# A fused attention, mixture-of-experts and gated-network kernel: two unused tiles that shift SBUF addresses, and raw weight loads issued one step earlier

## The chip, the cores and the metric

The kernel runs on one core of one Trainium2 chip. The metric is the device time of one execution in microseconds (us). Several executions were timed, and one execution was also recorded by the hardware profiler; the rows below come from that one.

## What is computed

Three stages follow each other, with float32 inputs and outputs, except that weights of the last network lie in HBM as 64-bit floats.

```python
# 1. attention: 4 batches, 8 heads, 512 local and 32 global positions, head size 64
s_g = scale * q_g @ concat(k_g, k_l).T ; out_g = softmax(s_g) @ concat(v_g, v_l)
s_l = concat(scale * q_l @ k_g.T, where(|i - j| <= 32, scale * q_l @ k_l.T, -1e9))
out_l = softmax(s_l) @ concat(v_g, v_l)
x = concat(out_g, out_l) as (4, 544, 512)
# 2. mixture of 8 experts, one expert per token, 512 -> 1024 -> 512
e = argmax(logits[b, s]) if s == 0 or local_gate[b, s] < 0.5 else previous e
out[b, s] = p[e] * (relu(x[b, s] @ w1[e]) @ w2[e])
# 3. network with a gate, 512 -> 1024 -> 512
h = relu(x @ w_in)
gate = sigmoid(conv_out)      # depthwise, 3 taps along the sequence
return (h * gate) @ w_out
```

## The kernel before

Attention fills about the first 160 us, the mixture of experts the time to about 430 us, the last network the rest. Large products are done in three passes: each float32 operand is split into a high part (suffix h) and a residual (suffix l), and PE multiplies high by high, high by residual and residual by high. A split is a cast on ACT (line 1043 for weights) and a subtraction on DVE (line 1044 for weights, line 1101 for tokens). Three lines hold 432 such matmuls of full tiles each (144 for each pass): L1108 (first layer of an expert, stationary xh or xl), L1124 (second layer of an expert, stationary gh or gl) and L1625 (second layer of the last network, stationary fh or fl). 128 rows of a stationary operand lie at the same byte address in 128 partitions.

**The mixture of experts** sorts the tokens by expert into slots of at most 128, 25 at most; `Moe.step(s)` (line 1405) handles one slot, `Moe.run` (line 1185) calls it for s = 2 to 20. A step does, in this order: first layer of slot s (`layer1`), the load of the next first-layer weights (`fetch(s, 1)`, 2 MB, only if the expert changes), a gather of tokens for slot s+3, the transposition of the tokens of slot s+1, the finishing operation of a conversion that waits (line 1017), the split of the next first-layer weights (`resplit(s + 1, 1)`), a conversion (only if the expert does not change), second layer of slot s-1 (`layer2`), the load of the next second-layer weights (`fetch(s - 1, 2)`, 2 MB, under the same condition), the transposition of the hidden values of slot s, the split of the second-layer weights (`resplit(s, 2)`), and a conversion (if the expert changes). Slots with few tokens take a short path through the unsplit weights, `few`. The conditions are read from memory at run time and appear as branches (L1294, L1303).

**The raw pieces.** The weights of the last network arrive as 64-bit floats in 16 pieces of 128 rows by 4 KB (0.52 MB each). `raw_load` (line 1441) puts a piece into one half of the tile fx, the halves by turns; `convert` calls `conv64` (lines 1006 to 1017), which makes float32 of it by integer operations: six on DVE (L1010 to L1015, 128 x 512 each), one on POOL (L1016), and the finishing one on DVE (L1017), deferred to the next step. In the kernel before, piece s-3 is loaded at the head of step s and converted in step s.

**Queues.** All these loads are issued by SP, in program order; an issue that has to wait holds up everything behind it on SP. Weight loads go to the tiles ws1 (first layer) and ws2 (second layer). `Ffn2.open` (line 1485) makes the tiles of the last network, the main function at line 1716 those of constants.

Of the kernel before, what the change touches and what calls it, by code (L numbers as in the profile page):

```python
# [8 lines left out]
F32 = mybir.dt.float32  # L9
F32R = mybir.dt.float32r  # L10
BF16 = mybir.dt.bfloat16
I32 = mybir.dt.int32
# [5 lines left out]
P = 128  # L18
# [69 lines left out]
class Attn:  # L88
    def __init__(self, ctx, cr, cs, tc, q_l, k_l, v_l, q_g, k_g, v_g, wcat, wz, ident, x_dram, L, late, hook):
        self.tc, self.nc = tc, tc.nc  # L90
        nc = tc.nc
        self.q_l, self.k_l, self.v_l, self.q_g, self.k_g, self.v_g = q_l, k_l, v_l, q_g, k_g, v_g
        self.wcat, self.ident, self.x_dram, self.L, self.late, self.hook = wcat, ident, x_dram, L, late, hook
        self.lgt, self.wz = {}, wz
# [247 lines left out]
    def evac(self, c, ps, tag, w=P):  # L342
# [4 lines left out]
        if c < B:  # L347
            j = 4 * c + c // 2
            nc.vector.tensor_copy(self.L[:, j:j + 4, :], t.rearrange("p (i e) -> p i e", e=32)[:, :, 0:9])
        else:  # L350
            nc.vector.tensor_copy(self.L[0:w, 8, :], t[0:w, 0:9])

# [207 lines left out]
NA = 2  # L560
# [95 lines left out]
class Routing:  # L656
    def __init__(self, nc, c, pool, ident, L):
        self.nc, self.c, self.ident, self.L = nc, c, ident, L
        self.m = pool.tile([P, NT], F32, name="r_m")
# [275 lines left out]
    def few(self, b0, first):  # L935
# [3 lines left out]
        v.scalar_tensor_tensor(sm, b0, -128.0, first[0:1], ALU.mult, ALU.add)  # L939
        v.tensor_scalar(sm, sm, P - TS - 0.5, 1024.0, ALU.is_lt, ALU.mult)  # L940
        v.tensor_tensor(sm, sm, b0, ALU.add)
# [37 lines left out]
        v.tensor_tensor(self.gate, pg, rx, ALU.mult)  # L979


TS = 32
NTS = P // TS
NWARM_M = 10
# [21 lines left out]
def conv64(nc, raw, out):  # L1006
    hi, lo = raw[:, :, 1], raw[:, :, 0]
    v = nc.vector
    a = out.bitcast(I32)
    v.tensor_scalar(a, hi, 3, 0x7FFFFFFF, ALU.logical_shift_left, ALU.bitwise_and)  # L1010
    v.scalar_tensor_tensor(a, hi, -2 ** 31, a, ALU.bitwise_and, ALU.bitwise_or)
    v.tensor_scalar(hi, hi, 1, 21, ALU.logical_shift_left, ALU.logical_shift_right)
    v.tensor_scalar(hi, hi, 897.0, -1.0, ALU.is_ge, ALU.mult)
    v.scalar_tensor_tensor(a, lo, 29, a, ALU.logical_shift_right, ALU.bitwise_or)
    v.tensor_scalar(lo, lo, 28, 1, ALU.logical_shift_right, ALU.bitwise_and)  # L1015
    nc.gpsimd.tensor_tensor(a, a, lo, ALU.add)  # L1016
    return lambda: v.scalar_tensor_tensor(a, a, 0x40000000, hi, ALU.bitwise_xor, ALU.bitwise_and)  # L1017
# [33 lines left out]
class Moe:  # L1051
    def __init__(self, sig, tc, W, ident, x_dram, y_dram, rt, w1, w2, wi, wo):
        self.nc, self.tc = tc.nc, tc
        self.W, self.ident, self.x_dram, self.y_dram = W, ident, x_dram, y_dram
        self.rt, self.w1, self.w2, self.wi, self.wo = rt, w1, w2, wi, wo
        self.sig = sig
        self.xs, self.xt, self.ht, self.hs, self.next, self.chg, self.sm = {}, {}, {}, {}, {}, {}, {}
        self.conv = []

    def open(self, ctx):  # L1060
        self.ctx = ctx
        self.tp = ctx.enter_context(self.tc.tile_pool(name="m_tp", bufs=2))
        self.ps = ctx.enter_context(self.tc.tile_pool(name="m_ps", bufs=2, space=PSUM))
        self.ys = [self.tp.tile([P, DM], F32, name=f"ys{i}", bufs=1) for i in range(2)]
# [243 lines left out]
    def turn_x(self, s):  # L1308
# [13 lines left out]
        def raw():  # L1322
            nc.scalar.copy(xs[:, 0:NKC * TS].rearrange("p (k t) -> p k t", t=TS), t[:, :, P - TS:P])  # L1323

# [15 lines left out]
    def layer1(self, s):  # L1340
# [4 lines left out]
        def few():  # L1345
            w = FF // NTS
            for k in range(NKC):
                for j in range(NTS):
                    nc.tensor.matmul(hp[0][TS * j:TS * j + TS, 0:w], xs[:, TS * k:TS * k + TS], W.s[1][:, k, w * j:w * j + w],
                                     start=k == 0, stop=k == NKC - 1)  # L1350
# [31 lines left out]
    def layer2(self, s):  # L1382
# [5 lines left out]
        def few():  # L1388
            for k in range(NFC):
                j, a = divmod(k, n)  # L1390
                for i in range(NTS):
                    nc.tensor.matmul(yp[TS * i:TS * i + TS, 0:w], hs[:, P * (n + a) + TS * j:P * (n + a) + TS * j + TS],
                                     W.s[2][:, k, w * i:w * i + w], start=k == 0, stop=k == NFC - 1)
            for i in range(NTS):
                nc.scalar.copy(y[P - TS:P, w * i:w * i + w], yp[TS * i:TS * i + TS, 0:w])

# [7 lines left out]

    def step(self, s):
        W, hi = self.W, NSLOT - 3
        if NA < s <= NA + 16:
            self.raw_load(s - NA - 1)
        if s + 1 < hi - 1:
            self.small(s + 1)  # L1410
        self.layer1(s)
        self.fetch(s, 1)
        if s + 3 < hi:
            self.xs[s + 3] = self.gather(s + 3)
        if s + 1 < hi - 1:
            self.turn_x(s + 1)
        else:
            self.xt[s + 1] = self.hi_lo_t(self.xs.pop(s + 1), NKC, "x")
        while self.conv:
            self.conv.pop()()  # L1420
        self.resplit(s + 1, 1)
        if NA < s <= NA + 16:
            with self.tc.If(self.chg[s + 1] == 0):
                self.convert(s - NA - 1)
        if s == NA:
            for _ in self.rest:
                pass
        else:
            self.layer2(s - 1)
            self.fetch(s - 1, 2)  # L1430
        self.turn_h(s)
        self.resplit(s, 2)
        if NA < s <= NA + 16:
            self.conv.pop()
            with self.tc.If(self.chg[s + 1] != 0):
                self.convert(s - NA - 1)
# [2 lines left out]
        return (1, s // 2, 512 * (s % 2)) if s < 8 else (2, s - 8, 0)  # L1439

    def raw_load(self, s):
        self.raw = self.f2.fx[s % 2].bitcast(I32).rearrange("p (n t) -> p n t", t=2)
        n, k, o = self.chunk(s)
        src = (self.wi, self.wo)[n - 1]
        self.nc.sync.dma_start(self.raw.rearrange("p n t -> p (n t)"), src[P * k:P * k + P, 2 * o:2 * o + 1024])

    def convert(self, s):
        n, k, o = self.chunk(s)
        self.conv.append(conv64(self.nc, self.raw, self.W.f[n][:, k, o:o + 512]))


class Ffn2:
# [32 lines left out]
    def open(self, ctx):  # L1485
        nc, tc = self.nc, self.tc
        self.tp = ctx.enter_context(tc.tile_pool(name="f_tp", bufs=2, reuse_waits="tile"))
        self.ps = ctx.enter_context(tc.tile_pool(name="f_ps", bufs=2, space=PSUM, reuse_waits="tile"))
        self.hp = [self.tp.tile([P, S + 2], F32, name=f"f_hp{i}", bufs=1) for i in range(3)]
        for t in self.hp:  # L1490
            nc.gpsimd.memset(t[:, 0:1], 0.0)
            nc.gpsimd.memset(t[:, S + 1:S + 2], 0.0)
        self.n = 0
# [207 lines left out]
def moe_kernel(ctx, tc, q_l, k_l, v_l, q_g, k_g, v_g, w_gate, w_local, w1, w2, w_in, conv_w, w_out, out):  # L1701
    nc = tc.nc
    outf = out.rearrange("b s d -> (b s) d")
    with tc.manual_schedule():
        cp = ctx.enter_context(tc.tile_pool(name="const", bufs=1))
# [8 lines left out]
        warm = cp.tile([P, 1], F32, name="warm")  # L1714
        nc.scalar.activation(warm, ident[:, 0:1], AF.Exp)
        L = cp.tile([P, NT, 9], F32, name="L")
        cc = Consts()

        def late():
# [142 lines left out]
```

## Time and profile before

| what | value |
|---|---|
| time, median of 3 runs | 636.39 us (634.14 to 636.82) |
| the profiled execution | 638.55 us |
| its span in the profile | 636.6 us |
| mean granted clock of TensorE | 0.979 |
| busy: PE, PEld, DVE, ACT, POOL | 92%, 77%, 66%, 50%, 27% of the span |

The span is what the profiler recorded between the first and the last instruction; the execution's own time is 1.95 us longer. PE is the engine of matmuls, PEld its loads of stationary operands, DVE, ACT and POOL are VectorE, ScalarE and GpSimd, SP issues DMAs; a q behind a name (PEq, DVEq, SPq) is the engine's sequencer, which handles branches, waits and issues. [...]

### The profile page before, as it was taken

Reading aid. Unit: us, or ns where it says so; the run is one execution under the profiler, and the core shown is the slowest. Engines: PE = TensorE matmul, PEld = TensorE weight load, DVE = VectorE, ACT = ScalarE, POOL = GpSimd, SP = SyncE. Lnnn points to the kernel's source line nnn. Section 1 sums busy time; section 2 is a strip of 40 time slices with the busy share of each in tenths; the row PEclk is TensorE's granted clock in tenths of the full one; section 3 lists DMA queues with packets and bytes.
Section 4 is the critical chain, followed back from the end, with each engine's and each line's share of the span. In section 5 each row is a group of like instructions: output and inputs, shape, how many; then the busy total and the mean of one; then the engine's idle time right before and its main releaser. Section 6 shows DMA issues by size and latency. Waiting matters only on the chain. (4 is left out here: it accounts for less than half of the span.)

```text
span 636.6 us, 16330 instructions
## 1 busy us (share of the span) xinstructions
PE 587.8 (92%) x6066; PEld 487.0 (77%) x6066; DVE 417.0 (66%) x868; ACT 317.6 (50%) x634; POOL 174.4 (27%) x226
## 2 busy tenths in 40 slices
PE   8879888889989999969989899969899999999997
PEld 6667666666758888758777688749898998998986
DVE  7778477865965867775687884676993293293340
ACT  5755455564225454451454743655863464363331
POOL 7665810042031422323233430100042132300100
PEclk9999799998899999999999999998999999999999
DMA  9989858557139666575466664023101201000001
GB/s 233 199 207 246 205 126 206 183 184 260 56 89 323 241 210 232 176 275 200 143 217 233 223 245 150 32 88 86 51 1 50 82 3 49 34 2 34 33 34 49
DMA packets 60643, 90.56 MB, mean 142 GB/s; under 512 B 25726, under 2 KB 34198, under 8 KB 60504
## 3 DMA queue, kind: packets, MB, share of 16 engines
q1 hardware_dynamic: 57016, 78.93, 40.4%
q0 software_dynamic: 3520, 10.23, 4.9%
q8 instruction: 64, 1.05, 0.7%
q14 instruction: 43, 0.35, 0.2%
HBM read 125.87 MB, written 15.79 MB: 223 GB/s over the span
## 5 line engine op out<-in xcount | busy, mean ns | idle before, releaser
L1567 DVE SCALAR_TENSOR_TENSOR fc<-f_hp,cw,fc 128x544 f32<-128x544 f32 (+2 forms) x66 | 51.4, 779 | 71.8 <-ACT fc L1565 70.4
L1044 DVE TENSOR_TENSOR wl<-ws,wh 128x512 fp32r<-128x512 f32 (+1 forms) x92 | 74.3, 868 | 12.8 <-ACT wh L1043 11.9
L1043 ACT CAST wh<-ws 128x512 fp32r<-128x512 f32 (+1 forms) x96 | 66.2, 772 | 1.6 <-ACT xs L1323 0.6
L1124 PE MATMUL yp<-wh,gh 128*128 128x512 f32 x144 | 59.8, 415 | 1.1 <-ACTq L1294 0.9
L1124 PE MATMUL yp<-wl,gh 128*128 128x512 f32 x144 | 57.6, 400 | 0.7 <-DVEq L1294 0.7
L1108 PE MATMUL hp<-wl,xh 128*128 128x512 f32 x144 | 48.8, 411 | 10.2 <-DVEq L1294 7.5
L1124 PE MATMUL yp<-wh,gl 128*128 128x512 f32 x144 | 57.6, 400 | 0.0
L1625 PE MATMUL f<-wh,fh 128*128 128x512 f32 (+1 forms) x144 | 55.4, 385 | 0.0
L1625 PE MATMUL f<-wl,fh 128*128 128x512 f32 (+1 forms) x144 | 55.0, 382 | 0.0
L1625 PE MATMUL f<-wh,fl 128*128 128x512 f32 (+1 forms) x144 | 55.0, 382 | 0.0
L1081 POOL DMA_INDIRECT y_dram<-ys,sidx x22 | 25.7, 1170 | 99.3 <-ACT ys L1400 48.3
L1272 ACT ACTIVATE hs<-hp 128x512 f32<-128x512 f32 x36 | 19.9, 595 | 64.8 <-PE hp L1108 64.8
L1108 PE MATMUL hp<-wh,xh 128*128 128x512 f32 x144 | 50.1, 419 | 0.1
L278 ACT ACTIVATE pr<-sp,nm 128x128 f32<-128x128 f32 x128 | 36.5, 375 | 24.5 <-DVE nm L275 24.5
L1108 PE MATMUL hp<-wh,xl 128*128 128x512 f32 x144 | 48.0, 405 | 0.0
L1069 POOL DMA_INDIRECT xs<-x_dram,gidx x22 | 27.0, 1227 | 67.3 <-ACT pr L278 35.2
L1108 PEld LDWEIGHTS hp<-wl,xh 128*128 128x128 f32 x144 | 27.7, 196 | 18.4 <-DVEq L1294 8.8
L1016 POOL TENSOR_TENSOR wf<-wf,fx 128x512 int32<-128x512 int32 x16 | 20.9, 1307 | 75.8 <-DVE fx L1015 64.5
L1572 ACT ACTIVATE f_hp<-f 128x544 f32<-128x544 f32 x31 | 19.3, 624 | 34.2 <-PE f L1548 34.1
L1634 ACT COPY fy<-f 128x512 f32<-128x512 f32 (+1 forms) x18 | 10.1, 563 | 48.5 <-PE f L1625 48.5
L1400 ACT COPY ys<-yp 128x512 f32<-128x512 f32 x15 | 8.8, 587 | 50.7 <-PE yp L1124 43.5
L1108 PEld LDWEIGHTS hp<-wh,xl 128*128 128x128 f32 x144 | 28.0, 195 | 7.0 <-DVE xl L1101 0.2
(380 smaller groups left out, 1528.3 us busy)
## 6 DMA issues: line engine op xcount, KB each, us to landing
ws<-in_moe_w_dram SPq DMA_DIRECT2D x42, 2048.0 KB
fx<-y_dram SPq DMA_DIRECT2D x17, 256.0 KB
raw<-in_k_l_dram SPq DMA_DIRECT2D x16, 256.0 KB
x_dram<-x SPq DMA_DIRECT2D x16, 256.0 KB
fx<-in_moe_w_in_dram SPq DMA_DIRECT2D x8, 512.0 KB
fx<-in_moe_w_out_dram SPq DMA_DIRECT2D x8, 512.0 KB
out_dram<-fy SPq DMA_DIRECT2D x16, 256.0 KB
VA<-in_v_l_dram SPq DMA_DIRECT2D x20, 192.0 KB
```

The lines of the kernel that those rows point to most:

```text
L278: nc.scalar.activation(pr[:, hp, :], sp[:, hp, :], AF.Exp, bias=nm[:, hp:hp + 1], scale=-1.0)
L1016: nc.gpsimd.tensor_tensor(a, a, lo, ALU.add)
L1043: (cp.tensor_copy if cp else self.nc.scalar.copy)(h, src[n][:, k, :])
L1044: eng.tensor_tensor(l, src[n][:, k, :], h.bitcast(F32), ALU.subtract)
L1069: self.nc.gpsimd.indirect_dma_start(out=xs, out_offset=None, in_=self.x_dram[0:n, :], in_offset=bass.IndirectOffsetOnAxis(ap=self.rt.gidx[ ...
L1081: self.nc.gpsimd.indirect_dma_start(out=self.y_dram[:, :], out_offset=bass.IndirectOffsetOnAxis(ap=self.rt.sidx[:, s:s + 1], axis=0), in_= ...
L1108: self.nc.tensor.matmul(hp[c], a[:, k, :], b[:, 512 * c:512 * c + 512], start=k == 0 and m == 0, stop=k == NKC - 1 and m == 2)
L1124: self.nc.tensor.matmul(yp, a[:, k, :], b, start=k == 0 and m == 0, stop=k == NFC - 1 and m == 2)
L1272: self.nc.scalar.activation(hs[:, 512 * c:512 * c + 512], hp[c], AF.Relu)
L1567: nc.vector.scalar_tensor_tensor(c[:, a:b], hp[:, a + t:b + t], self.cw[:, t, f:f + 1], c[:, a:b], ALU.mult, ALU.add)
L1572: self.nc.scalar.activation(hp[:, 1:S + 1].rearrange("p (a c) -> p a c", a=2), p[:, :, 0:272], AF.Relu)
L1625: self.nc.tensor.matmul(yp[:, cs], x[:, c], w[:, cs], start=f == 0 and n == 0, stop=f == NFC - 1 and n == 2)
```

## The change

Two parts. First, two tiles are made that nothing reads or writes: `pad_c` (104 floats, 416 bytes in each partition) behind L in the pool of constants, and `pad_f` (8 floats, 32 bytes) ahead of all others in the pool of the last network. Tiles that are placed after them move. The rows that PE loads as stationary operands start here (bytes modulo 512; "0 or 32" is what remains modulo 64):

```
tile             before   after   modulo 64
qT (batch 0, 2)     448     448   0  -> 0
qT (batch 1, 3)     288     192   32 -> 0
pr                  416     320   32 -> 0
xh, xl, gh, gl      320     224   0  -> 32
hs, xs              320     224   0  -> 32
wh1, wl1 (L1548)    480     480   32 -> 32
fh, fl (L1625)      288     224   32 -> 32
```

Second, the raw loads move. `step` no longer loads piece s-3 at its head; it loads piece s-2 behind the finishing operation of the waiting conversion, ahead of the second-layer part. The piece is converted in the next step, so `self.raw` now keeps each piece under its number.

```diff
--- before.py
+++ after.py
@@ -979,6 +979,7 @@
         v.tensor_tensor(self.gate, pg, rx, ALU.mult)
 
 
+PAD_C, PAD_F = 104, 8
 TS = 32
 NTS = P // TS
 NWARM_M = 10
@@ -1055,7 +1056,7 @@
         self.rt, self.w1, self.w2, self.wi, self.wo = rt, w1, w2, wi, wo
         self.sig = sig
         self.xs, self.xt, self.ht, self.hs, self.next, self.chg, self.sm = {}, {}, {}, {}, {}, {}, {}
-        self.conv = []
+        self.conv, self.raw = [], {}
 
     def open(self, ctx):
         self.ctx = ctx
@@ -1404,8 +1405,6 @@
 
     def step(self, s):
         W, hi = self.W, NSLOT - 3
-        if NA < s <= NA + 16:
-            self.raw_load(s - NA - 1)
         if s + 1 < hi - 1:
             self.small(s + 1)
         self.layer1(s)
@@ -1418,6 +1417,8 @@
             self.xt[s + 1] = self.hi_lo_t(self.xs.pop(s + 1), NKC, "x")
         while self.conv:
             self.conv.pop()()
+        if s < NA + 16:
+            self.raw_load(s - NA)
         self.resplit(s + 1, 1)
         if NA < s <= NA + 16:
             with self.tc.If(self.chg[s + 1] == 0):
@@ -1439,14 +1440,14 @@
         return (1, s // 2, 512 * (s % 2)) if s < 8 else (2, s - 8, 0)
 
     def raw_load(self, s):
-        self.raw = self.f2.fx[s % 2].bitcast(I32).rearrange("p (n t) -> p n t", t=2)
+        raw = self.raw[s] = self.f2.fx[s % 2].bitcast(I32).rearrange("p (n t) -> p n t", t=2)
         n, k, o = self.chunk(s)
         src = (self.wi, self.wo)[n - 1]
-        self.nc.sync.dma_start(self.raw.rearrange("p n t -> p (n t)"), src[P * k:P * k + P, 2 * o:2 * o + 1024])
+        self.nc.sync.dma_start(raw.rearrange("p n t -> p (n t)"), src[P * k:P * k + P, 2 * o:2 * o + 1024])
 
     def convert(self, s):
         n, k, o = self.chunk(s)
-        self.conv.append(conv64(self.nc, self.raw, self.W.f[n][:, k, o:o + 512]))
+        self.conv.append(conv64(self.nc, self.raw[s], self.W.f[n][:, k, o:o + 512]))
 
 
 class Ffn2:
@@ -1486,6 +1487,7 @@
         nc, tc = self.nc, self.tc
         self.tp = ctx.enter_context(tc.tile_pool(name="f_tp", bufs=2, reuse_waits="tile"))
         self.ps = ctx.enter_context(tc.tile_pool(name="f_ps", bufs=2, space=PSUM, reuse_waits="tile"))
+        self.tp.tile([P, PAD_F], F32, name="pad_f", bufs=1)
         self.hp = [self.tp.tile([P, S + 2], F32, name=f"f_hp{i}", bufs=1) for i in range(3)]
         for t in self.hp:
             nc.gpsimd.memset(t[:, 0:1], 0.0)
@@ -1714,6 +1716,7 @@
         warm = cp.tile([P, 1], F32, name="warm")
         nc.scalar.activation(warm, ident[:, 0:1], AF.Exp)
         L = cp.tile([P, NT, 9], F32, name="L")
+        cp.tile([P, PAD_C], F32, name="pad_c")
         cc = Consts()
 
         def late():
```

SP in step 8 and at the head of step 9, before. The two loads into ws are the next first-layer weights and the next second-layer weights, the load into fx is raw piece 6, and an ISA row is the register work of a conditional load:

```order
L1036 ISA
L1036 DMA ws_3446<-in_moe_w_dram 128x4x1024 [waits DVE_49,DMAHW6_49,PE_49,Activation_49]
L1294 UNCONDITIONAL_BRANCH
L1423 UNCONDITIONAL_BRANCH
L1303 UNCONDITIONAL_BRANCH x2
L1036 ISA
L1036 DMA ws_2723<-in_moe_w_dram 128x8x512 [waits DVE_49,DMAHW7_49,PE_49,Activation_49]
L1445 DMA fx<-in_moe_w_in_dram 128x1024 [waits DMAHW5_49,DVE_49]
L1294 UNCONDITIONAL_BRANCH
L1435 UNCONDITIONAL_BRANCH
```

The same place with the change (line numbers are one higher):

```order
L1037 ISA
L1037 DMA ws_3447<-in_moe_w_dram 128x4x1024 [waits DVE_49,DMAHW6_49,PE_49,Activation_49]
L1446 DMA fx<-in_moe_w_in_dram 128x1024 [waits DMAHW4_49,DVE_49]
L1295 UNCONDITIONAL_BRANCH
L1424 UNCONDITIONAL_BRANCH
L1304 UNCONDITIONAL_BRANCH x2
L1037 ISA
L1037 DMA ws_2724<-in_moe_w_dram 128x8x512 [waits DMAHW0_49,PE_49,Activation_49]
```

The load of piece 6 stood behind both loads into ws and stands between them now; what it waits for on DVE is the finishing operation of the conversion before. PE, ACT, DVE and POOL have the same instructions in the same order as before.

## Rows read from the trace of the kernel before

**Rows 1.** The page: span, and part 1, busy time by engine.

```profile
span 636.6 us, 16330 instructions
...
PE 587.8 (92%) x6066; PEld 487.0 (77%) x6066; DVE 417.0 (66%) x868; ACT 317.6 (50%) x634; POOL 174.4 (27%) x226
```

**Rows 2.** Waits of PE, 160 to 431 us: waited for, us, times, longest.

```profile
PE hp L1108 <- DVEq L1294: 7.5, 3, 4.7
```

**Rows 3.** Line 1010 (conversion's first operation): idle before it, us, times.

```profile
  DVEq L1294: 4.6, 15
  DMA fx<-in_moe_w_in_dram: 3.4, 1
```

**Rows 4.** Timeline, 255 to 285 us: start us, us, engine, line, xcount, [idle before <-releaser].

```profile
255.40 6.45 SPq L1036 DMA_DIRECT2D ws<-in_moe_w_dram  x2
...
257.29 0.69 DVE L1017 SCALAR_TENSOR_TENSOR wf<-wf,fx 128x512 int32<-128x512 int32 x1 [1.22 <-DVEq L1303]
...
261.95 0.52 SPq L1445 DMA_DIRECT2D fx<-in_moe_w_in_dram  x1
...
269.24 0.69 DVE L1017 SCALAR_TENSOR_TENSOR wf<-wf,fx 128x512 int32<-128x512 int32 x1
...
271.71 4.27 ACT L1043 CAST wh<-ws 128x512 fp32r<-128x512 f32 x8 [0.49 <-DMA ws<-in_moe_w_dram]
...
273.30 0.43 DVE L1010 TENSOR_SCALAR wf<-fx 128x512 int32<-128x512 int32 x1 [3.37 <-DMA fx<-in_moe_w_in_dram]
...
277.01 5.59 DVE L1044 TENSOR_TENSOR wl<-ws,wh 128x512 fp32r<-128x512 f32 x8 [0.56 <-ACT hs L1272]
...
283.56 0.69 DVE L1101 TENSOR_TENSOR xl<-xlp,xh 128x512 fp32r<-128x512 f32 x1 [0.95 <-DVEq L1435]
...
284.96 1.09 PE L1108 MATMUL hp<-wl,xh 128*128 128x512 f32 x2 [4.73 <-DVEq L1294]
```

**Rows 5.** Windows: us, busy of PE, PEld, DVE, ACT, POOL, PEclk, DMA, GB/s.

```profile
257.00:261.40 4.40, 4.40 (x22) 3.52 (x21) 4.11 (x5) 3.56 (x4) 0.00 (x0) 1.00 0.21 63
285.00:288.40 3.40, 3.40 (x8) 2.63 (x9) 3.00 (x6) 0.00 (x0) 0.10 (x1) 0.52 0.98 302
288.40:329.40 41.00, 40.94 (x275) 32.41 (x273) 26.44 (x41) 19.01 (x37) 14.05 (x12) 1.00 0.51 172
331.00:336.00 5.00, 4.97 (x21) 4.06 (x22) 4.29 (x8) 0.00 (x0) 1.46 (x2) 1.00 0.97 348
364.10:367.40 3.30, 3.30 (x9) 2.64 (x10) 3.30 (x3) 0.75 (x2) 1.95 (x1) 0.55 1.02 372
```

**Rows 6.** Timeline: two other restarts of PE after a pause.

```profile
331.03 0.74 PE L1108 MATMUL hp<-wl,xh 128*128 128x512 f32 x2 [1.62 <-DVEq L1294]
...
364.08 1.22 PE L1108 MATMUL hp<-wl,xh 128*128 128x512 f32 x2 [2.76 <-DVE wl L1044]
```

**Rows 7.** Timeline, 357 to 379 us: second-layer load, raw piece 15, first cast.

```profile
357.40 3.85 SPq L1036 DMA_DIRECT2D ws<-in_moe_w_dram  x2
...
362.92 0.34 SPq L1445 DMA_DIRECT2D fx<-in_moe_w_out_dram  x1
...
378.40 2.20 ACT L1043 CAST wh<-ws 128x512 fp32r<-128x512 f32 x4
```

**Rows 8.** Timeline: score matmuls (L267) of the second and third batch.

```profile
42.41 1.13 PE L267 MATMUL sp<-kT,qT 64*32 64x128 f32 x64
...
96.53 1.13 PE L267 MATMUL sp<-kT,qT 64*32 64x128 f32 x64
```

**Rows 9.** Timeline: matmuls of L1124 and of L1625, first and last counted.

```profile
264.72 0.40 PE L1124 MATMUL yp<-wl,gh 128*128 128x512 f32 x1
...
269.88 0.39 PE L1124 MATMUL yp<-wh,gl 128*128 128x512 f32 x1
...
616.71 0.39 PE L1625 MATMUL f<-wh,fl 128*128 128x512 f32 x1
...
627.21 0.40 PE L1625 MATMUL f<-wh,fl 128*128 128x512 f32 x1
```

## The prediction

> **What bounds the kernel now.** I read the page's busy shares first, then PE's waits, then the line that ends the longest of them, then the timeline around it, and last the granted clock by stretches. PE is busy 92% of the 636.6 us span [rows 1], so what counts is the rest of PE's time and PE's pace. In the stretch of the mixture of experts (160 to 431 us) the dearest wait of PE is L1108 on DVE's queue, 7.5 us in 3 times, one of them 4.7 us [rows 2]. Line 1010, the first operation of a conversion of a raw piece, tells why: 15 of its 16 calls waited for nothing but a branch, 4.6 us together, and one waited 3.4 us for the raw load itself [rows 3].
>
> The timeline shows that one [rows 4]. The issue row that begins at 255.40 holds two weight loads: the first-layer load of step 8 and, ending at 261.85, the second-layer load. Raw piece 6 is issued right behind, at 261.95. DVE is through with the finishing operation of piece 5 at 269.24 + 0.69 = 269.93, then has nothing until 273.30: 3.37 us, released by the DMA into fx. From there the chain has no room: the six operations end 0.56 us before 277.01, the eight residuals of the second layer's weights take 5.59 us, xl is made at 283.56, and PE takes up L1108 at 284.96 after 4.73 us of nothing. So PE was free from 284.96 - 4.73 = 280.23.
>
> The stall has a tail. [...] Two other restarts of PE stand beside it [rows 6]: after 1.62 us of nothing (331.03) the clock stays at 1.00, after 2.76 us (364.08) it is 0.55 in the next 3.3 us [rows 5].
>
> **The change part by part.** *The raw load one step earlier.* The order of SP shows piece 6 between the first-layer load and the second-layer load of step 8, where it was behind both. It must wait there for the finishing operation of that step, which frees its half of fx: 257.29 + 0.69 = 257.98 [rows 4]. From 257.0 to 261.4 the DMA engines are 0.21 busy and move 63 GB/s [rows 5]. The piece has 0.52 MB: 1.7 us at the 302 GB/s of the stretch from 285.0, 8.3 us even at 63 GB/s, which is 259.7 to 266.3. It is wanted at 269.93 + 0.23 = 270.16 at the soonest (0.3 us, 4.6 over 15, is what the branch costs the others [rows 3]; I take 0.23). So this wait goes: 273.30 - 270.16 = **3.14 us**.
>
> Does the rest follow? The residuals would begin at 273.87; ACT begins the casts that they read at 271.71 and ends all eight 4.27 us later, at 0.53 us each against 0.70 us for a residual [rows 4], so it stays ahead. xl comes at 280.42, PE resumes at 281.82. It still has nothing to do for 4.73 - 3.14 = **1.59 us**: this is what is late next, the DVE chain itself. In the 41 us after 288.4 PE has 0.06 us free while DVE works 26.44 us and the DMA engines are half busy (0.51) [rows 5]; what feeds PE there has room and follows it, so the 3.14 us reach the end.
>
> *The clock.* 1.59 us is less than the 1.62 us that left the clock up, so I take it to stay at 1.00 after 281.82. What the low stretch costs now: 3.4 us at 0.52 instead of 1.00 is 3.4 x 0.48 = **1.6 us**. With the pause this close to the only pause that is known harmless, the bound on the other side is nothing.
>
> *The other 15 pieces* win nothing at their conversions, as none waited for data. What they do to the second-layer loads: each raw load now stands ahead of one, and in it waits for DVE's finishing operation, so the second-layer load queues on SP behind that wait and on the DMA engines behind 0.52 MB. The tightest case I found: a second-layer load whose issue ends at 357.40 + 3.85 = 361.25 and whose cast begins at 378.40 [rows 7]. Today's raw piece 15 is issued right after the finishing operation of the step, at 362.92, so the moved piece could go then and the load 0.3 us later. Both are 2.62 MB: at 302 GB/s they have landed 8.7 us on, at 371.6, at the 172 GB/s of the quiet 41 us at 378.1 [rows 5]. Both ends lie before 378.40, so I charge **nothing**; the cover is 0.3 to 6.8 us, and where it is gone each microsecond late is one of PE's. The order of PE, DVE, ACT and POOL does not change, and the number of instructions does not.
>
> *The two pads.* No instruction comes or goes; stationary rows start elsewhere. By the placement table, rows that began on a multiple of 64 bytes now begin 32 past one (xh, xl, gh, gl, hs), others go the other way (qT1, pr, pts), fh and fl keep 32. The trace of before holds both kinds. The 64 score matmuls of two batches, one with stationary rows 32 past (qT1, at 42.41) and one on the multiple (qT0, at 96.53), both take 1.13 us [rows 8], equal to 0.2 ns each. For three-pass matmuls, L1124 (on the multiple) makes 22 intervals from 264.72 to 269.88, 234.5 ns each; L1625 (32 past) 45 from 616.71 to 627.21, 233.3 ns each [rows 9]. There are 1,296 such matmuls in L1108, L1124 and L1625, so 1.2 ns either way are -1.6 to +1.6 us. I take zero, nearest to both pairs.
>
> The sum: -3.14 - 1.63 + 0 + 0 = **-4.8 us**. The profiled execution, 638.55 us, becomes 633.8. It stood 2.2 us above the median of the runs, 636.39, which becomes **631.6 us**.
>
> **The rivals.** *A. Only the wait goes, the clock falls all the same.* For it: 1.59 us against 1.62 us is no margin, one row bears it. Against: 2.76 us is the shortest pause seen to cost clock here. Gain 3.1 us, 633.3 us.
>
> *B. No gain.* The moved load is held back on SP (the first-layer load ahead of it, or the wait for the finishing operation of step 8) until it runs beside the 2 MB load again; or PE, which finishes 3 us sooner, meets the next wait for weights 3 us sooner. Against: the DMA engines' 63 GB/s before 261.4 [rows 5], and PE's 41 full microseconds after. 636.4 us.
>
> *C. Rows that start in the right place make matmuls quicker.* In the trace L1625's 233.3 ns are the best that rows show, and its start class is the one that xh and gh now get. If more of a row's place counts than the 64-byte class (the starts go from 320 to 224 modulo 512) and it gives 3 ns on each of 1,296, that is 3.9 us more: 627.7 us.
>
> *D. Slower: the new start costs PE.* The same mechanism the other way: x and g rows leave a 64-byte multiple. It overtakes the gain and the 0.5% (3.2 us, about what a measurement of this kernel can tell from no change) from (4.8 + 3.2)/1,296 = 6.2 ns a matmul; at 8 ns it is 10.4 - 4.8, so 642.0 us. Against it stands the 1.13 us of rows 8, and that L1625 is no slower.
>
> *E. Slower: a second-layer load comes too late.* The issue order on SP decides: behind a 0.52 MB piece and its wait the load has at most 6.8 us of cover in the tightest place [rows 5, 7]. To eat 4.8 us and 3.2 us more it would have to land 14.8 us later than the 371.6 worked out; two or three such places would do it with half of that: 640 us. Now the rows: piece 6 was issued behind a 2 MB load, and DVE saw it 11.35 us later (273.30), while the 2 MB ahead were cast from 271.71 [rows 4]. That is transfer in the order of issue. [...]
>
> **How the numbers follow.** The forecast as summed, 631.6 us, gets 0.62 (its own range, with the pads' bounds, 630.0 to 633.2). A 0.12, B 0.10, C 0.07, D 0.07, E 0.02. A lies on the line of 0.5% (633.2): I count 0.05 of it as faster, 0.07 as same, and 0.03 of the forecast's as same. Faster: 0.59 + 0.07 + 0.05, about 0.70; same: 0.03 + 0.07 + 0.10, about 0.21; slower 0.09. The range goes down to 627.5 us, to take in C, and up to 636.0 us, which takes in A and those parts of B that gain something; outside stay the rest of B, D and E, and a little below, under 0.2.
>
> **What would show it.** Right: L1010 waits for no DMA in any of 16 calls; PE's longest wait of L1108 on DVE's queue is about 1.6 us instead of 4.7; the clock in the 3.4 us after that restart is near 1.00; L1124 and L1625 keep 234.5 and 233.3 ns; casts of the second-layer weights wait for no DMA. Wrong: a DMA wait at L1043 or at another L1010, a restart at 0.5 clock (A), a pace of L1108, L1124 or L1625 off by more than 1.2 ns (C or D), or a change of the time that lies in the last network, which neither moved loads nor this stall touch.

## The result and the profile after

| | before | with the change |
|---|---|---|
| median of 4 runs each | 636.61 us (634.14 to 637.46) | 627.33 us (626.84 to 627.80) |
| ratio, 95% interval | | 0.9861 (0.9824 to 0.9897) |
| profiled execution, its span | 638.55, 636.6 us | 626.94, 624.9 us |

The change is faster by 1.4%, about 9 us, where 4.8 were forecast. 627.33 us lies 0.2 us under the low end of the range, 627.5. The direction came as forecast, the size was nearly double. A second set of runs of the same kernel (`r_after` below) gave 0.9877 (0.984 to 0.9915), about 8 us. Medians here count every run; ratios leave out runs in a slower state (805 to 933 us at a granted clock of 0.56 to 0.65 of full speed, and one of 643.56 us), so a ratio is not the quotient of two medians.

The page, span and busy times, as in [rows 1]:

```profile
span 624.9 us, 16315 instructions
...
PE 579.3 (93%) x6066; PEld 484.7 (78%) x6066; DVE 416.5 (67%) x868; ACT 318.2 (51%) x634; POOL 176.5 (28%) x226
```

PE's waits between 160 and 431 us (waited for, total, times, longest), as in [rows 2]. The longest one on DVE's queue fell from 4.7 to 2.2 us; the one for wl, 2.76 us before [rows 6], is 3.1:

```profile
PE hp L1109 <- DVEq L1295: 5.4, 3, 2.2
PE hp L1109 <- DVE wl L1045: 3.1, 1, 3.1
```

The first operation of a conversion (now line 1011), idle time before it, as in [rows 3]: all 16 wait for a branch only, none for the DMA.

```profile
  DVEq L1295: 4.9, 16
```

The place of the stall in the timeline, as in [rows 4], and one later restart of PE:

```profile
251.23 0.69 DVE L1018 SCALAR_TENSOR_TENSOR wf<-wf,fx 128x512 int32<-128x512 int32 x1 [1.22 <-DVEq L1304]
...
251.95 0.34 SPq L1446 DMA_DIRECT2D fx<-in_moe_w_in_dram  x1
...
263.18 0.69 DVE L1018 SCALAR_TENSOR_TENSOR wf<-wf,fx 128x512 int32<-128x512 int32 x1
...
264.28 0.43 DVE L1011 TENSOR_SCALAR wf<-fx 128x512 int32<-128x512 int32 x1 [0.41 <-DVEq L1295]
...
265.57 4.27 ACT L1044 CAST wh<-ws 128x512 fp32r<-128x512 f32 x8 [0.73 <-DMA ws<-in_moe_w_dram]
...
267.99 5.59 DVE L1045 TENSOR_TENSOR wl<-ws,wh 128x512 fp32r<-128x512 f32 x8 [0.57 <-PE hp L1109]
...
274.54 0.69 DVE L1102 TENSOR_TENSOR xl<-xlp,xh 128x512 fp32r<-128x512 f32 x1 [0.95 <-ACTq L1295]
...
275.94 0.72 PE L1109 MATMUL hp<-wl,xh 128*128 128x512 f32 x2 [2.21 <-DVEq L1295]
...
321.69 0.73 PE L1109 MATMUL hp<-wl,xh 128*128 128x512 f32 x2 [2.09 <-DVEq L1295]
```

Raw piece 6 is issued at 251.95, right behind the finishing operation of its step. The finishing operation of the next step ends at 263.87, and the conversion begins at 264.28, after 0.41 us of waiting for the branch, instead of after 3.37 us of waiting for the DMA. ACT's casts begin at 265.57, the residuals at 267.99. PE's pause is 2.21 us instead of 4.73; 1.59 were forecast.

The clock behind that restart and behind the later one, as in [rows 5] (us, busy of PE, PEld, DVE, ACT, POOL, PEclk, DMA, GB/s):

```profile
275.90:279.30 3.40, 3.36 (x9) 2.66 (x10) 3.01 (x6) 0.00 (x0) 0.01 (x1) 0.61 0.68 182
321.70:326.70 5.00, 5.00 (x22) 4.16 (x23) 4.29 (x8) 0.00 (x0) 1.50 (x2) 1.00 0.72 224
```

The clock fell here all the same, to 0.61 in 3.4 us (0.52 before [rows 5]), while it stayed at 1.00 behind the pause of 2.09 us at 321.69.

The pace of the three-pass matmuls, as in [rows 9], line 1125 (was L1124) and line 1627 (was L1625):

```profile
258.73 0.40 PE L1125 MATMUL yp<-wh,gl 128*128 128x512 f32 x1
...
263.51 0.39 PE L1125 MATMUL yp<-wh,gl 128*128 128x512 f32 x1
...
604.00 0.39 PE L1627 MATMUL f<-wh,fl 128*128 128x512 f32 x1
...
613.97 0.39 PE L1627 MATMUL f<-wl,fh 128*128 128x512 f32 x1
```

The pace is the time from the start of one matmul to the start of the next. From 258.73 to 263.51 are 21 intervals, 227.6 ns each; from 604.00 to 613.97 are 44, 226.6 ns each. Before it was 234.5 and 233.3 ns. This the forecast had at zero.

Not all of the 11.6 us between the two profiled executions is the change's. The last attention matmul of one group starts at 150.2 us before, at 145.2 after, and at 150.5 in `e4_scan_w` below, whose tiles of attention lie where the change has them; the same view of the three, in this order (engine, operation, count, ns min/median/max, first and last start):

```profile
L300 PE MATMUL op<-VC,pts x384: 217/220/318, 18.8 to 150.2; 128*32 128x65 f32 x192
```

```profile
L300 PE MATMUL op<-VC,pts x384: 217/220/317, 18.2 to 145.2; 128*32 128x65 f32 x192
```

```profile
L300 PE MATMUL op<-VC,pts x384: 217/220/317, 17.8 to 150.5; 128*32 128x65 f32 x192
```

So attention moves by some 5 us from execution to execution, and effects of under 5 us are read from runs in rounds or from the time behind attention. Whether the pads, which move tiles of attention too, change anything there is not shown: without them it ends at 147.0 (`d1_dist256`) to 150.2.

### The profile page after: what moved, and what is told of

It is laid out like the page before. It is cut to its first block, busy times and chain, and to the rows that moved or that the text cites. A ratio compares the mean times of both kernels' runs of the same rounds, so it can differ in the third digit from the quotient of the medians.

```text
span 624.9 us, 16315 instructions
## 1 busy us (share of the span) xinstructions
PE 579.3 (93%) x6066; PEld 484.7 (78%) x6066; DVE 416.5 (67%) x868; ACT 318.2 (51%) x634; POOL 176.5 (28%) x226
## 3 DMA queue, kind: packets, MB, share of 16 engines
q1 hardware_dynamic: 57016, 78.93, 41.7%
## 5 line engine op out<-in xcount | busy, mean ns | idle before, releaser
L1125 PE MATMUL yp<-wh,gh 128*128 128x512 f32 x144 | 58.9, 409 | 1.1 <-ACTq L1295 0.9
L1125 PE MATMUL yp<-wl,gh 128*128 128x512 f32 x144 | 57.0, 396 | 0.7 <-DVEq L1295 0.7
L1125 PE MATMUL yp<-wh,gl 128*128 128x512 f32 x144 | 57.0, 396 | 0.0
L1109 PE MATMUL hp<-wl,xh 128*128 128x512 f32 x144 | 47.5, 402 | 8.6 <-DVEq L1295 5.4
L1627 PE MATMUL f<-wh,fh 128*128 128x512 f32 (+1 forms) x144 | 54.8, 380 | 0.0
L1627 PE MATMUL f<-wh,fl 128*128 128x512 f32 (+1 forms) x144 | 54.4, 378 | 0.0
L1627 PE MATMUL f<-wl,fh 128*128 128x512 f32 (+1 forms) x144 | 54.4, 378 | 0.0
```

Source lines behind the costliest of these rows:

```text
L1109: self.nc.tensor.matmul(hp[c], a[:, k, :], b[:, 512 * c:512 * c + 512], start=k == 0 and m == 0, stop=k == NKC - 1 and m == 2)
L1125: self.nc.tensor.matmul(yp, a[:, k, :], b, start=k == 0 and m == 0, stop=k == NFC - 1 and m == 2)
L1627: self.nc.tensor.matmul(yp[:, cs], x[:, c], w[:, cs], start=f == 0 and n == 0, stop=f == NFC - 1 and n == 2)
```

## The experiments

Each was compared with the kernel before on the same chip; times are medians. The pace in the tables is the mean of the start-to-start intervals of a line that lie between 200 and 245 ns (351 to 378 intervals a line), worked out from the start times in the traces.

**e1_pads: the two unused tiles alone.**

```diff
+PAD_C, PAD_F = 104, 8
+        self.tp.tile([P, PAD_F], F32, name="pad_f", bufs=1)
+        cp.tile([P, PAD_C], F32, name="pad_c")
```

> The kernel before with the two unused tiles and nothing else. Theory P (the place where a stationary row starts sets the pace of a 512-column three-pass matmul, and the tiles gave the change some 4 to 5 us of its 9): L1124, L1108 and L1625 come every 227 to 229 ns as in the changed kernel, not 233 to 234, the first operation of one conversion still waits about 3.4 us for its raw load, and the time is 630 to 633 us. Rival N (the quicker pace belongs to the execution or the chip, not to the tiles): 233 to 234 ns and 636 to 637 us.

Measured: 632.13 us against 637.59, ratio 0.9927 (0.9894 to 0.9961). Pace 228.7 ns in L1108, 228.5 in L1124, 227.7 in L1625. The stall (the conversion that waits for its raw load) is there, both in the idle time before L1011 and in PE's waits:

```profile
  DVEq L1295: 4.5, 15
  DMA fx<-in_moe_w_in_dram: 2.8, 1
```

```profile
PE hp L1109 <- DVEq L1295: 7.5, 3, 4.5
```

Tiles that nobody reads or writes are worth 4.7 us (0.73% of 637.59), as theory P says; its reason, the place of the stationary row alone, is refuted further down.

**e2_raw: the raw loads alone**, the diff of the change without the three lines above.

> The change without the two tiles: raw loads one step earlier alone. Theory P: the pace stays at 233 to 234 ns, no first operation of a conversion waits for a DMA, the longest wait of PE's L1108 on DVE's queue is 1.6 to 2.2 us instead of 4.7, and the time is 632 to 634 us (3 to 4.8 us less than before). Rival R (the move of the loads brought all of it): 627 to 628 us with a pace of 227 ns. Rival 0 (the stall comes back elsewhere): 636 us.

Measured: 632.03 us against 637.59, ratio 0.9922 (0.9886 to 0.9957), 5.0 us (2.7 to 7.3). Pace 234.0, 234.0 and 233.3 ns, as before. Idle before L1010, the conversion and PE's restart at the place of the stall, and the clock behind it:

```profile
  DVEq L1294: 4.7, 15
  DVE wf L1017: 0.2, 1
```

```profile
267.81 0.43 DVE L1010 TENSOR_SCALAR wf<-fx 128x512 int32<-128x512 int32 x1 [0.42 <-DVEq L1294]
...
279.47 0.74 PE L1108 MATMUL hp<-wl,xh 128*128 128x512 f32 x2 [1.78 <-DVEq L1294]
```

```profile
279.50:282.90 3.40, 3.40 (x15) 2.76 (x16) 3.00 (x6) 0.00 (x0) 0.09 (x1) 1.00 0.72 217
```

The DMA wait is gone, PE's pause is 1.78 us, and the clock stays at 1.00. This is the forecast's case; its pause of 1.59 us came out 0.19 longer, because the branch ahead of the conversion cost 0.42 us and not 0.23.

**r_after: the change once more, in five rounds**, the same file.

> The changed kernel once more, beside the kernel before in five rounds. The raw loads alone gave a ratio of 0.9922 and the two tiles alone 0.9927; if the two gains simply add, the ratio is 0.985; if they overlap (from the end of attention to the last matmul of L1625 the tiles took 3.4 us off, the raw loads 5.7, both together 7.1), about 0.989.

Measured: 628.30 us against 637.70, ratio 0.9877 (0.984 to 0.9915). The estimate lies on the overlapping side, but the interval still holds the plain product, 0.985. PE's restart and the clock behind it:

```profile
277.38 0.81 PE L1109 MATMUL hp<-wl,xh 128*128 128x512 f32 x2 [1.96 <-DVEq L1295]
```

```profile
277.40:280.80 3.40, 3.40 (x9) 2.69 (x10) 3.01 (x6) 0.00 (x0) 0.06 (x1) 0.57 0.70 221
```

A pause of 1.96 us, and the clock at 0.57. One part of the overlap is shown in this: with the tiles PE comes to the same wait earlier, DVE does not. From the first operation of that conversion to PE's restart DVE's chain takes 11.66 us in the kernel before (273.30 to 284.96), in e2_raw (267.81 to 279.47) and in the change (264.28 to 275.94). So the pause is longer than in e2_raw, and the clock that e2_raw keeps is lost. Two kernels below agree: d1_dist256 (moved loads, quick pace) pauses 2.05 us and has 0.59 in the 3.4 us behind it, d2_dist352 (moved loads, old pace) 1.78 us and 1.00.

**e3_scan_f: 24 tiles of f, each starting 32 bytes further than the last modulo 512.**

```diff
-self.tp.tile([P, S + 3 * SG], F32R, tag="f" + x
+self.tp.tile([P, S + 3 * SG + 8], F32R, tag="f" + x
```

> The changed kernel with the 12 + 12 tiles of fh and fl 32 bytes longer each, so that their rows start in all 16 multiples of 32 modulo 512 in one run; wh2 and wl2, which move past them, stay at 480. Theory P: the intervals of L1625 differ by tile, 227 ns where a row starts at 224 and 233 where it starts at 288, 4 ns or more between the best and the worst start. Rival N: all tiles within 1.5 ns of each other.

Measured: 633.13 us in one run. The mean pace of L1625 went from 227.5 to 231.4 ns. Sorted by the stationary row's own start, the intervals have no simple order: tiles at 224 came every 231.7 ns on average, not 227, those at 448 every 229.9, those at 32 every 233.8. What one tile gets in a mixed stream says little about a stream in which all start alike: even in the changed kernel a group of L1627 begins with intervals of mostly 224 to 236 ns, and only from the tenth on is every one 226 to 228. Theory P in its simple form (a good start is good) did not pass.

**e4_scan_w: eight starts for wh1 and wl1.**

```diff
-hl.tile([P, w], F32R, name=f"w{x}{n}_{k}") for x in "hl")
+hl.tile([P, w + 8 * (2 - n)], F32R, name=f"w{x}{n}_{k}")[:, 0:w] for x in "hl")
```

> The changed kernel with the eight tiles wh1 and wl1 32 bytes longer each: their rows start at 224, 256, ... 448 modulo 512 instead of all at 480. They are stationary in L1548 (272 columns, 125 ns in both kernels so far) and pass by in L1108. Theory P: the intervals of L1548 differ by tile, by half as much as for 512 columns or more (2 to 8 ns), and those of L1108 do not change with the start of what passes by. Rival (the two starts count together): L1108's intervals change with the start of wh1 and wl1 too, with xh and xl at 224 as they are. Rival N: 125 ns in L1548 and 227 in L1108 everywhere.

Measured: 632.99 us in one run. In L1548 medians ran from 120 to 132 ns by the pair of starts and the pass (high part, rows passing by at 352 and stationary at 320: 120 to 121; 160 and 416: 130), and the same pair and pass gave nearly the same median in other batches, whose tiles lie at quite other addresses. The pair alone does not fix it: 160 and 416 gave 130 ns with the high part passing by and 124 to 125 with the residual; what else counts no run shows. Over all pairs the mean stayed at about 126 ns. L1108, whose xh and xl had not moved, went from 228.6 to 232.1 ns. So the two starts count together, and the next two kernels were made to tell how.

**d1_dist256 and d2_dist352: the rows that pass by are moved instead.** An unused tile behind the split weights; d1 is on e2_raw, d2 on the change.

```diff
         for n, nk, w in ((1, NKC, FF), (2, NFC, DM)):
             self.t[n] = [...]
+        hl.tile([P, 104], F32, name="pad_w")    (d1; 24 in d2)
```

> The kernel with the raw loads moved and without the two tiles (x, g rows at 320, f at 288 modulo 512), but with an unused tile of 416 bytes behind the split weights, so that wh and wl of both layers start at 64 instead of 480. Theory D (the distance between the start of the stationary rows and the start of the rows that pass by decides): the distance in L1108 and L1124 is 320 - 64 = 256, as in the changed kernel (224 - 480), so they come every 227 ns, and the time is 3 to 5 us under the 632.0 us of the raw loads alone. Theory A (the stationary rows' own start decides): 234 ns and 632 us. L1625 gets a distance of 224, which has not been seen: no number for it.

> The changed kernel (x, g, f rows at 224) with an unused tile of 96 bytes behind the split weights, so that wh and wl start at 384 instead of 480. Theory D: the distance is 224 - 384 = 352 modulo 512, as in the kernel before in L1108 and L1124, so L1108, L1124 and L1625 come every 234 ns and the time goes back to 631 to 633 us. Theory A: 227 ns and 627 to 628 us.

Measured, d1: 629.65 us against 637.36, ratio 0.9877 (0.9821 to 0.9934); d2: 632.33 us, ratio 0.9913 (0.9871 to 0.9955). The same stretch of line 1124 (now L1125 in d1, L1126 in d2), first and last of 21 intervals, d1 and then d2:

```profile
259.88 0.40 PE L1125 MATMUL yp<-wh,gl 128*128 128x512 f32 x1
...
264.67 0.40 PE L1125 MATMUL yp<-wh,gl 128*128 128x512 f32 x1
```

```profile
265.06 0.40 PE L1126 MATMUL yp<-wh,gl 128*128 128x512 f32 x1
...
269.98 0.40 PE L1126 MATMUL yp<-wh,gl 128*128 128x512 f32 x1
```

That is 228.1 ns with x and g rows at 320, where they make 234 ns in the kernel before, and 234.3 ns with rows at 224, where they make 227 ns in the change. Theory A falls, theory D holds in these streams, whose tiles all start alike: the mean pace went with the **distance** between the start of the stationary rows and the start of the rows that pass by, modulo 512 bytes, 228.1 ns at 256 and 234.3 at 352. The time of d1 came 2.4 us under e2_raw's 632.03 where 3 to 5 were expected, and the two intervals overlap; what tells the theories apart is the pace.

**s1_scan and s2_scan: six more distances**, by other sizes of the unused tiles and one ahead of x and one behind wl1.

```diff
-PAD_C, PAD_F = 104, 8
+PAD_C, PAD_F = 72, 72      (s2: 88, 32)
+                self.tp.tile([P, 56], F32, name="pad_x", bufs=1)      (s2: 32)
+            if n == 1:
+                hl.tile([P, 40], F32, name="pad_w")      (s2: 64)
```

> The changed kernel with other sizes of unused tiles: x at 320 with wh1 and wl1 at 320 (distance 0), g at 96 with wh2 and wl2 at 480 (distance 128), f at 352 with 480 (distance 384). [...] Theory A: x at 320 gives 234 ns as in the kernel before.

> The same with x at 288 and wh1, wl1 at 224 (distance 64), g at 160 (distance 192 to 480), f at 256 (distance 288 to 480). Theory D: three paces, each the same over its line. Theory A: x at 288 gives 233 ns as f at 288 did in the kernel before.

Measured: 635.15 and 631.49 us in one run each. All distances together, for streams that start alike:

```
distance   0     64    128   192   224   256          288   320   352          384
ns       228.3  233.3  232.3 229.5 233.4 227.5-228.8  233.2 233.3 233.9-234.3  232.2
from      s1     s2     s1    s2    d1   change, d1    s2   before before, d2    s1
```

0, 192 and 256 are the good ones of the ten seen; none was better than the change's own 256, so no better place came out of it. Six of the sixteen multiples of 32 were not tried. The three pairs that lie 256 apart (0 and 256, 64 and 320, 128 and 384) agree within 0.8 ns, so a period of 256 bytes fits the ten as well as one of 512.

**r_double: every raw piece loaded twice**, one load behind the other into the same half.

> The changed kernel with each raw piece loaded twice into its half of fx, the second load behind the first, so that every second-layer load stands on SP behind two pieces of 0.52 MB and the wait between them, some 3 to 6 us later than in the changed kernel. Theory C (second-layer loads have cover): the same time within 1 us, casts of second-layer weights wait for DMA 1 to 3 us more in the one tight step. Rival E (the cover is used up already): each microsecond of the later load shows, 3 us or more over several steps.

Measured: 662.33 us, ratio 1.0427 (1.0375 to 1.048). SP's waits (the second copy waits for the first to land) and ACT's idle time before the casts of weights, and the latter in the changed kernel:

```profile
SPq L1447 <- DMA fx<-in_moe_w_in_dram: 58.9, 8, 11.0
SPq L1447 <- DMA fx<-in_moe_w_out_dram: 39.3, 8, 8.0
```

```profile
  DMA ws<-in_moe_w_dram: 41.7, 6
```

```profile
  DMA ws<-in_moe_w_dram: 0.9, 2
```

The extra wait was 98.2 us in 16 times, 6.1 us on average and up to 11.0; casts then waited 41.7 us in 6 places, and the kernel lost 34 us against 628.30. Rival E is right about this kernel: the loads behind the doubled pieces are no longer covered. The second copies are also 16 x 0.52 = 8.4 MB more to move; no run separates that from the waiting on SP. In the changed kernel itself the casts wait 0.9 us in 2 places, where the kernel before has 0.5 us in one.

**k_pool: two of eight second-layer residuals on POOL**, `POOL_K = {1: (), 2: (3, 7)}`.

> The changed kernel with two of the eight residuals of a second-layer split (chunks 3 and 7) on POOL instead of DVE. In the three places where PE still waits for DVE (2.2, 2.1 and 3.1 us) eight residuals of 0.70 us stand in DVE's chain; two fewer are 1.4 us less in each. If DVE's chain is what is late next: the three waits shrink to about 0.8, 0.7 and 1.7 us, 4 us in all, and the clock stays up behind them, 622 to 625 us. Rival: POOL's residuals (about 1.2 us each by the 2.4 us that a 1024-column one takes) come later than DVE's or slow DVE beside them, and nothing is won.

Measured: 637.35 us, ratio 1.0023 (0.9993 to 1.0052): all of the gain is gone. DVE's residuals of 512 columns in this kernel and in the changed one (count, busy us, mean ns, idle before), and PE's waits:

```profile
L1045 DVE TENSOR_TENSOR wl<-ws,wh 128x512 fp32r<-128x512 f32 x52 | 50.3, 1020 | 7.3 <-ACT wh L1044 5.9 <-PE hp L1109 1.1 <-ACTq L1295 0.2
```

```profile
L1045 DVE TENSOR_TENSOR wl<-ws,wh 128x512 fp32r<-128x512 f32 x64 | 41.9, 715 | 7.2 <-ACT wh L1044 6.5 <-PE hp L1109 0.6
```

```profile
PE hp L1109 <- DVEq L1295: 8.2, 3, 3.6
PE hp L1109 <- DVE wl L1045: 5.0, 1, 5.0
```

The mean of DVE's residuals goes from 715 to 1,020 ns. It is not a slower pace of all: by the start times, the ten that run beside one of POOL's residuals take 683 to 3,490 ns, 2,229 on average, and the 16 that run while POOL does nothing take 685, as in the changed kernel (683). PE's waits grow from 2.2 to 3.6 us and from 3.1 to 5.0. The rival is right.

**k_fill: unused matmuls in front of PE's pauses.**

```diff
+            for _ in range(12):
+                nc.tensor.matmul(yp[:, w:2 * w], self.ident, self.ident, start=True, stop=True)
```

> The changed kernel with twelve unused matmuls of 128 columns (about 1.3 us at full clock, identity by identity into unread columns of yp) at the end of the short second layer, which stands ahead of each of the three pauses of PE behind 270 us (2.0 to 2.2, 2.1 and 3.1 us in the two traces of the changed kernel). Theory G (PE's pause is what the clock falls for, the rest of the chain is DVE's and does not move): the pauses are 1.2 to 1.4 us shorter, the restart that now runs at 0.61 of the full clock runs at 1.00, as the 1.62 us pause of the kernel before did, and the time is 1 to 3 us less than the changed kernel (the fourth short slot, where PE does not wait, costs 1.3 us). Rival H (the clock falls at this place for another reason, or what PE does late makes DVE or ACT late): the same clock, and 1 to 4 us more.

Measured: 628.68 us, ratio 0.9872 (0.9828 to 0.9916), the same as the change, not the 1 to 3 us less of theory G. The twelve became 24 records and 2.94 us instead of 1.3, and filled the pauses of 2.2 and 2.1 us whole and the one of 3.1 but for 0.7; the clock is 1.00 throughout:

```profile
277.27 2.94 PE L1396 MATMUL yp<-ident 128*128 128x128 f32 x24
```

```profile
270.00:300.00 30.00, 30.00 (x214) 25.45 (x213) 20.07 (x35) 12.43 (x27) 10.81 (x10) 1.00 0.60 205
300.00:340.00 40.00, 40.00 (x312) 32.43 (x311) 31.06 (x45) 22.11 (x39) 12.34 (x11) 1.00 0.58 204
340.00:380.00 40.00, 39.34 (x256) 32.85 (x255) 33.69 (x55) 22.01 (x42) 13.80 (x10) 1.00 0.62 223
```

With the pause filled the clock stayed at 1.00 at this place in this one trace, where it was 0.61 and 0.57 in the two of the change (as theory G had it), but the time is no better. That the fillers cost what the clock gives back is likely, as 2.94 us is more than two of the pauses were (2.0 to 2.2 us) and a fourth slot had none; it was not measured by itself, and fewer fillers were not tried.

## Why the prediction was right, and where it was wrong

**The stall: right.** The one conversion that waited for its data waits no more, in the change and in e2_raw. Forecast was 3.14 us less pause for PE; e2_raw shows 4.73 - 1.78 = 2.95, r_after 2.77, the change's own trace 2.52. The 0.19 us that e2_raw lacks are the branch, taken at 0.23 us and measured at 0.42. The whole forecast, 4.8 us, is what the moved loads are worth alone: 5.0 us.

**The clock: right alone, wrong in the change.** The forecast took a pause of 1.59 us and a clock that stays up, 1.6 us won. In e2_raw it is so (1.78 us, 1.00), with some luck: 1.78 is over the 1.62 us on which the forecast leaned. In the change the pause is 2.21 us in one execution and 1.96 in the other, and the clock was 0.61 and 0.57 in the 3.4 us behind it: 3.4 x 0.39 = 1.3 and 3.4 x 0.43 = 1.5 us of the 1.6 are given back. The step that failed is the pause: it was worked out with PE's old pace, and a quicker PE only waits longer for DVE. Rival A had the fallen clock, for want of margin and not for that reason. The length of the pause does not decide alone: at this place the clock stayed at 1.00 behind 2.01 us in s1_scan and was 0.59 behind 2.01 us in e3_scan_f, and in the change it stayed up behind 2.09 us at 321.69. What decides is open.

**The two pads: wrong.** "I take zero, nearest to both pairs" is the step that failed, with bounds of 1.6 us either way; e1_pads measured 4.7 us. It is the larger part of what the forecast missed. The bound compared L1124 and L1625 as two kinds of start (on a multiple of 64 and 32 past one). By the distance to the rows that pass by they are one kind: 320 - 480 is 352 modulo 512, 288 - 480 is 320, and both distances are slow, 234 and 233 ns. The trace of before held no fast stream, so no pair of its 512-column rows could have shown it; the score matmuls of [rows 8] are 128-column ones of another kind. Rival C named the outcome (a row's place counts, 3.9 us more) at 0.07; what it measured is 5.3 to 5.8 ns a matmul, not 3. (The 1,296 of the forecast are 1,248 matmuls of 512 columns and, in L1625, 48 of 256.) Worked out, 432 x 5.3 + 432 x 5.6 + 384 x 5.8 = 6.9 us; the 48 matmuls of 256 columns in L1625 went the other way, from 113 to 120 ns, 0.3 us. That only 4.7 of 6.6 us came out is explained in part: PE's three long pauses ahead of L1108 behind 270 us add up to 9.6 us in e1_pads against 9.1 before, and in the one trace of each the granted clock is 0.77 in the 15 us around the start of the last network (419 to 434) where it was 0.89 before (425 to 440). The interval of e1_pads (2.5 to 6.8 us) holds both numbers. The forecast's range came within 0.2 us of the result only because it was stretched down for rival C, whose reason, the start class that L1625 had, is not the one found. Two of the forecast's own signs of being wrong came true in the change: paces off by more than 1.2 ns (227.6 for 234.5 in L1124), and a restart with the clock down (0.61 in one trace, 0.57 in the other).

What the pace is made of can be seen a little further. The loads of the stationary rows last the same in both kernels by the median, the matmuls (whose ends the profile models) do not; first pass of L1108, before and after (ns min/median/max):

```profile
L1108 PEld LDWEIGHTS hp<-wh,xh x144: 186/188/337, 146.9 to 413.4; 128*128 128x128 f32 x144
...
L1108 PE MATMUL hp<-wh,xh x144: 391/400/775, 147.0 to 413.7; 128*128 128x512 f32 x144
```

```profile
L1109 PEld LDWEIGHTS hp<-wh,xh x144: 186/188/329, 142.7 to 403.2; 128*128 128x128 f32 x144
...
L1109 PE MATMUL hp<-wh,xh x144: 387/389/628, 142.7 to 403.4; 128*128 128x512 f32 x144
```

The median load has 188 ns in both; the median matmul beside it goes from 400 to 389 ns. Why the distance counts no run shows.

**The second-layer loads: nearly right.** Nothing was charged, and the casts waited 0.4 us more in all (1.2 more in r_after). The cover of 0.3 to 6.8 us came from one place, and how much other places have is not known: r_double, with 6.1 us more wait ahead of each load and twice the raw pieces to move, went past it in 6 places. Rivals B, D and E did not come true in the change.

## What to carry to other kernels

Where PE ran back to back with tiles that all start alike, the start of the stationary rows relative to the start of the rows that pass by was a knob of its own: unused tiles of 416 and 32 bytes took the pace from 234.5 to 227.6 ns in L1124 and from 233.3 to 226.6 in L1625, 2.9%. It was found by trying distances, not by reading one trace. Two streams with nearly the same pace were no proof that place does not matter: L1124 at 234 ns and L1625 at 233 were both of the slow kind (distances 352 and 320). Part of the gain on PE was lost where PE then waited for DVE, whose chain kept its 11.66 us: a pause of 1.78 us in e2_raw became 1.96 and 2.21 in the change, and the clock behind it 0.57 and 0.61 instead of 1.00.

## What had not been expected of the hardware

- The pace of fp32r matmuls of 512 columns (float32 operands in the type that PE reads for the passes) went from 227 to 234 ns with the distance of two start addresses modulo 512, or 256, at the ten distances seen; the same distance gave the same pace whichever operand moved (256: 227.6 ns in the change, 228.1 in d1; 352: 234.5 in the kernel before, 234.3 in d2). In the change's L1627 up to nine intervals of 224 to 236 ns stand ahead of those of 226 to 228.
- DVE's subtraction of 512 columns took 685 ns while POOL was idle (k_pool, 16 of them), and 683 to 3,490 ns when it overlapped one of POOL's subtractions (ten of them, mean 2,229).
- The same pause of PE, 2.01 us at the same place, was followed by a granted clock of 1.00 in s1_scan and 0.59 in e3_scan_f.
- The twelve matmuls of identity by identity in plain float32 of k_fill showed as 24 records, 2.94 us for the twelve.
